# A fused recurrence, MLP and gated-MLP kernel: the first MLP group split by chunk, block two's first product in float16 parts, the state's outer product inside the values' step

## The chip, the cores and the metric

The kernel runs on one core of a Trainium2 chip. The metric is the device time of one execution in microseconds (us). TensorE, here PE, multiplies; its weight loads are shown as a separate row, PEld. VectorE is DVE, ScalarE is ACT, GpSimd is POOL, and SyncE, whose queue starts the DMAs, is SP.

## The reference

Three stages follow each other. Batch is 2, sequence 768, 8 heads of 48, so the model's width is 384.

```python
def _attn_ref(r, k, v, w, u):
    state = np.zeros((B, H, D, D))
    for t in range(S):
        cur = np.einsum('bhd,bhe->bhde', u[None] * kt, vt)
        y[:, :, t] = np.einsum('bhd,bhde->bhe', rt, state + cur)
        state = wt[:, :, :, None] * state + np.einsum('bhd,bhe->bhde', kt, vt)

def _moe_ref(x, g_ln, w_ch1, w_ch2):          # 384 -> 1536 -> 384
    xn = (x - mu) / np.sqrt(var + 1e-06) * g_ln
    return x + np.maximum(xn @ w_ch1, 0.0) @ w_ch2

def _moe2_ref(x, w_in, w_spatial, b_spatial, w_out):   # 384 -> 1024
    h = np.maximum(x @ w_in, 0.0)
    u, v = h[..., :512], h[..., 512:]
    v_n = (v - mu) / np.sqrt(var + 1e-06)
    v_s = np.einsum('ts,bsd->btd', w_spatial, v_n) + b_spatial[None, :, None]
    return (u * v_s) @ w_out
```

The weights arrive as float64, and the kernel makes float32 of their bits by itself.

## The kernel before

The sequence is cut into 6 chunks of 128 tokens. A step i stands for chunk c and batch b, i = 2c + b, so there are 12. For each i the recurrence is done in chunk form: `prep` scans the decays forward and backward on DVE (tiles `Gs` and `E`) and multiplies them with the keys and receptances; `keys_t` transposes the keys on PE (`kT`), and ACT copies them (`kf`); `scores` multiplies keys with receptances (`sc`), and DVE masks the result (`am`); `values` forms the output of the chunk, for the first chunk from `am` alone (`y<-tk,am`), for later ones in three pieces, `inter` from the state (`y<-E,St`) and `intra(0)` and `intra(1)` from `am` (`y<-am,tk`); `state` forms the outer product of keys and values of the chunk for the next chunk's state (`stp<-tk,kf`) in a PSUM bank of its own turn; `norm` adds the term of `u` (`x`) and normalises (`st`, `k_var`, `sd`, `rs`, `xn`), where `sd` is ACT's square root; `turned` transposes `x` and `xn` on PE (`xT`, `xnT`) and ACT copies them to `x2v` and, for the first chunk, to `xfirst`.

The MLP (`moe1`) runs in six groups, one for each chunk of both batches, 256 tokens at a time. A group goes over 12 slices f of the hidden width: three products up (`pup`), a relu on ACT (`hh`), three products down that add up in two PSUM banks (`acc`). Group 0 multiplies float32 (`xfirst`, `w1f`, `w2f`), which shows in the trace as two records for a product. Groups 1 to 5 split each operand into two float16 parts and take three float16 products for one.

The weights come in 24 pieces of 384 KB (`raw<-in_w`), first w1's slice 0, then w2's slice 0, and so on. `convert` makes float32 of a piece: a shift (on DVE or ACT), a rebias on ACT, a sign and a merge on DVE (`w1f`, `w2f`), and later the two float16 parts.

Block two then forms `v` (`v_tile`, 12 tiles of 9 products, 512 wide) and `u` (`u_tile`, 16 tiles of 9 products, 384 wide) from `x2v`, split into two float32r parts `Xh` and `Xl`, and `w_in`, split into `winh` and `winl`; it normalises v, multiplies with the spatial weights (`sp_tile`, `p<-ws,vn`, float16 parts) and with `w_out` (`o_tile`).

The order of the work is not the order of the code. Every step is given to a planner (`Plan.add`) with its engine, a cost, a key and what it reads and writes; `Plan.order` then takes on each engine, whenever it is free, the ready step with the lowest key, and writes the instructions out in that order. The keys come from the table `PP`. On PE the planner puts small products of zeros (`pw<-warm`, 128 x 128 float16) into the time before the first MLP product wherever PE would stand idle, so that PE's clock stays up. A few sums of range checks (`k_max`, `k_var`, `k_sum`) decide at the end whether a slow general version is run instead; with these inputs it isn't.

Of the kernel before, what the change touches and what calls it, by code (L numbers as in the profile page):

```python
# [8 lines left out]
F32 = mybir.dt.float32  # L9
# [36 lines left out]
W_UP = 2.0 ** 8  # L46
S_UP = 2.0 ** 15
# [8 lines left out]
PP = {'SK': 12.413, 'SS': -5.481, 'RG': 987.703, 'HK': 188.98, 'HS': 3.199, 'HW': 3.533, 'SG': 'V', 'T0': 18.217, 'P': 68.821, 'H': 29.796, 'H0': 3.345, 'M0': -20.127, 'M0S': 16.711, 'AH': 55.305, 'AG': -2.079, 'US': 6.83, 'EV': 33.376, 'CV': 3.765, 'CS': 12.226, 'CW': 3.915, 'WK': 602.422, 'WS': 70.654, 'XK': 12.678, 'XS': 39.166, 'KG': 18.972, 'KU': 578.872, 'OK': 564.596, 'OS': 13.4, 'FG': 108.0, 'LOOK': 0.0, 'EK': 'V', 'EU': 'V', 'ER': 'V', 'RK': 'V', 'ED': 'V', 'SM': 'V', 'SH': 'AAVVVAVAAVAVAVVVA', 'LW': 'V', 'LX': 'V', 'LS': 'V', 'LV': 'V', 'LU': 'V'}  # L56
# [287 lines left out]
def tile_rwkv_moe_gmlp(ctx: ExitStack, tc: tile.TileContext, dt_in, tok_in, vg_in, u_in, g_in, w1_in, w2_in, win_in, wsp_in, b_in, wout_in, out, plan_only=False):  # L344
# [79 lines left out]
    k_max = const.tile([128, 10], F32, name="k_max")  # L424
    k_sum = const.tile([128, NCH], F32, name="k_sum")
# [44 lines left out]
    def load_d(i, key):  # L470
# [10 lines left out]
        if i < B:  # L481
            for n, (lo, hi, w) in enumerate(((2 * NP * C, DTC, "dw"), (NP * C, 2 * NP * C, "dk"), (0, NP * C, "dr"))):
                add("D", 750, key + 0.01 * n, part(lo, hi, not n), w=[(w, s)])
        else:
            add("D", 2250, key, part(0, DTC, True), w=[("dw", s), ("dk", s), ("dr", s)])

    def load_k(i, key):
# [7 lines left out]
        add("D", 640 * n // DM, key, fn, w=[("tv", i % 2), ("tr", i % 2)])  # L495
# [23 lines left out]
    def set_ud():  # L519
        G.memset(ud, 0.0)  # L520

# [13 lines left out]
    add("G", 42, -95, set_ud, w=["ud"])  # L535
# [13 lines left out]
    def convert(name, src, n, key, hi, lo, r_hi=(), w_hi=(), r_lo=(), w_lo=(), shape=None, lo_eng="G", sh="A", sg="V", whole=None, later=None):  # L549
# [15 lines left out]
        def rebias():  # L565

            e = words()[0].bitcast(F32)
            A.activation(out=e, in_=e, func=ACTF.Copy, scale=REBIAS * 2 if whole else REBIAS)  # L568
# [173 lines left out]
    def scores(i):  # L742
# [17 lines left out]
        add("T", 1090, ka(i, "sc"), sc, r=[("E", s), ("G", s), "att"], w=pp, use=0.42)  # L760
# [4 lines left out]
    def values(i):  # L765
# [50 lines left out]
        add("T", 4 * 125, ka(i, "ya"), inter, r=[("E", s), ("St", b), "att"], w=py, use=0.5)  # L816
        for e in range(2):
            add("T", 4 * 125, ka(i, "yb"), intra(e), r=[t["amt", i][e], ("tv", s), "att"], w=py, use=0.39)
# [20 lines left out]

    def state(i):  # L840
# [4 lines left out]
        p = bank("up" if i == 0 else "ys")  # L845

        def st():
            z = t["stp", i] = pst(p, f"stp{i}_")
            for h in range(H):
                lo, hi = halves[h % 2]  # L850
                sl = slice(D * h, D * h + D)
                mm(z[lo:hi, D * (h // 2):D * (h // 2) + D], t["kf", i][:, h // 2, lo:hi], t["tk", i][:, sl], True, True)
# [4 lines left out]
        add("T", 600, ka(i, "st"), st, r=[("kf", s), ("tv", s), "att"], w=[p], use=0.3)  # L857
# [5 lines left out]
    def norm_steps(n, x, pool, key, cols, mv, tok, extra, w_mv=()):  # L863
# [535 lines left out]
```

## Time and profile before

| | us |
|---|---|
| time, median of 3 runs (359.56 to 360.32) | 359.74 |
| the profiled execution's own time | 362.65 |
| its span, from first to last instruction | 360.9 |
| PE busy in the span | 351.7 |
| DVE busy | 283.6 |
| ACT busy | 155.3 |

The profiled execution took 362.65 us, 1.75 us more than its span, and 2.9 us more than the median of the runs without the profiler. PE's busy share is an upper bound of its use, since the small products of zeros count too. The stages from the span's start: the load and the first chunk until 33 us, then the MLP's groups with the recurrence between them until about 242 us, and block two until 354 us.

### The profile page before, as it was taken

How to read it: one execution, taken by the hardware profiler on the slowest of the kernel's cores; microseconds unless marked ns; L12 is line 12 of the kernel's file. 1: busy time of each engine (PE TensorE's matmuls, PEld its weight loads, DVE VectorE, ACT ScalarE, POOL GpSimd, SP SyncE). 2: the span in 40 equal slices, each digit the busy share in tenths (PEclk: the TensorE clock that was granted, in tenths of full speed). 3: DMA queues.
4: the chain of work that ended last, by engine and by line, in shares of the span. 5: the costliest groups of instructions: out<-in, count | busy, mean ns of one | idle time of the engine just before them, and what ended most of it. 6: DMA issues, size and time to landing. Idle time of an engine off the chain costs nothing.

```text
span 360.9 us, 7549 instructions
## 1 busy us (share of the span) xinstructions
PE 351.7 (97%) x3041; PEld 298.8 (83%) x3041; DVE 283.6 (79%) x675; ACT 155.3 (43%) x364; POOL 2.2 (1%) x22
## 2 busy tenths in 40 slices
PE   8989999999999999999999999999999999999992
PEld 8989887779888888888889888889765899965692
DVE  7969999999999999999999999999255783025500
ACT  1557988333232332423544765663421354211121
POOL 1000000000000000000000000000000000000000
PEclk9989999999999999999999999999999999999998
DMA  8999796132222541320101026601000000210021
GB/s 211 295 307 360 232 312 201 33 112 67 77 67 78 145 129 41 119 67 31 59 31 60 30 74 200 194 3 44 3 2 0 2 0 2 79 54 2 0 84 58
DMA packets 13022, 34.85 MB, mean 97 GB/s; under 512 B 1840, under 2 KB 3888, under 8 KB 12976
## 3 DMA queue, kind: packets, MB, share of 16 engines
q1 hardware_dynamic: 12976, 34.26, 30.4%
q8 instruction: 26, 0.43, 0.5%
q14 instruction: 20, 0.16, 0.1%
HBM read 31.90 MB, written 2.36 MB: 95 GB/s over the span
## 4 chain that ended last, share of the span: by engine, by line
PE 89%; DMA 7%; ACT 1%; SPq 1%; issue 0%; DVE 0%; ACTq 0%
PE p L394 34%; PE acc L394 21%; DMA raw<-in_w 5%; PE sc L394 3%; DMA tk<-in_tok 2%; PE kT L717 1%; SPq L478 1%; PE pup__641 L394 0%; PE y__996 L394 0%; PE pup__930 L394 0%; PE pup__804 L394 0%; PE pup__1051 L394 0%; PE pup__981 L394 0%; PE pup__845 L394 0%; PE pup__773 L394 0%; PE pup__750 L394 0%
## 5 line engine op out<-in xcount | busy, mean ns | idle before, releaser
L394 PE MATMUL acc<-hh,w2h 128*128 128x256 f16 x180 | 49.2, 273 | 0.0
L394 PE MATMUL acc<-hl,w2h 128*128 128x256 f16 x180 | 49.1, 273 | 0.0
L394 PE MATMUL acc<-hh,w2l 128*128 128x256 f16 x180 | 49.1, 273 | 0.0
L394 PE MATMUL p<-ws,vn 128*128 128x384 f16 x288 | 47.1, 326 | 0.0
L394 PEld LDWEIGHTS <-vn 128*128 128x128 f16 x288 | 28.0, 98 | 18.7 <-issue 0.4
L394 PEld LDWEIGHTS <-w2h 128*128 128x128 f16 x360 | 33.9, 98 | 6.3 <-issue 2.2
L394 PEld LDWEIGHTS <-w1h 128*128 128x128 f16 x360 | 34.9, 98 | 4.3 <-issue 0.2
L1224 DVE SCALAR_TENSOR_TENSOR misc<-p,misc 128x384 f32<-128x384 f32 x16 | 8.9, 558 | 30.6 <-PE p L394 30.6
L385 ACT ACTIVATE gh<-misc 128x384 fp32r<-128x384 f32 x16 | 8.4, 523 | 41.2 <-DVE misc L1225 41.2
L568 ACT ACTIVATE raw<-raw 128x384 f32<-128x384 f32 (+1 forms) x40 | 20.8, 524 | 4.3 <-DMA raw<-in_w 4.3
L574 ACT ACTIVATE raw<-raw 128x384 uint32<-128x384 uint32 (+1 forms) x31 | 15.9, 512 | 11.9 <-DMA raw<-in_w 11.9
L585 DVE SCALAR_TENSOR_TENSOR raw<-raw 128x384 int32<-128x384 int32 (+1 forms) x40 | 20.2, 511 | 0.4 <-ACT raw L568 0.3
L394 PE MATMUL pw<-warm 128*128 128x128 f16 x259 | 19.0, 242 | 1.1 <-DVE warm L499 1.1
L394 PEld LDWEIGHTS <-w2l 128*128 128x128 f16 x180 | 17.6, 98 | 2.1
L394 PEld LDWEIGHTS <-w1l 128*128 128x128 f16 x180 | 17.6, 98 | 2.1
L394 PEld LDWEIGHTS <-warm 128*128 128x128 f16 x259 | 18.0, 111 | 1.2 <-DVE warm L499 1.1
L394 PE MATMUL acc<-hh,w2f 128*128 128x256 f32 x72 | 17.9, 385 | 0.0
L388 DVE TENSOR_TENSOR gl<-misc,gh 128x384 fp32r<-128x384 f32 x16 | 8.9, 558 | 9.4 <-ACT gh L385 9.4
L394 PE MATMUL p<-woh,gl 128*128 128x384 f32 x48 | 16.3, 340 | 0.0
L394 PE MATMUL p<-woh,gh 128*128 128x384 f32 x48 | 16.2, 337 | 0.0
L394 PE MATMUL p<-xh,winh 128*128 128x384 f32 x48 | 16.2, 337 | 0.0
L394 PE MATMUL p<-wol,gh 128*128 128x384 f32 x48 | 16.1, 336 | 0.0
(702 smaller groups left out, 911.4 us busy)
## 6 DMA issues: line engine op xcount, KB each, us to landing
raw<-in_w SPq DMA_DIRECT2D x24, 384.0 KB, 7.2
dt<-in_dt SPq DMA_DIRECT2D x10, 675.5 KB, 5.3
tk<-in_tok SPq DMA_DIRECT2D x10, 576.0 KB, 3.7
raw<-in_win SPq DMA_DIRECT2D x12, 256.0 KB, 3.1
raw<-in_wsp SPq DMA_DIRECT2D x6, 384.0 KB, 3.4
out<-misc SPq DMA_DIRECT2D x12, 192.0 KB, 1.9
raw<-in_wout SPq DMA_DIRECT2D x4, 384.0 KB, 3.4
dt<-in_dt SPq DMA_DIRECT2D x4, 224.0 KB, 5.2
```

The source lines that it names most:

```text
L385: A.activation(out=out, in_=in_, func=ACTF.Copy)
L388: eng[e].tensor_tensor(out=out, in0=in0, in1=in1, op=ALU.subtract)
L394: T.matmul(out=out, lhsT=lhsT, rhs=rhs, start=start, stop=stop)
L478: Q.dma_start(out=t["dt", i][:, lo:hi], in_=dt_in[b, c, :, lo:hi])
L568: A.activation(out=e, in_=e, func=ACTF.Copy, scale=REBIAS * 2 if whole else REBIAS)
L574: A.activation(out=z, in_=z, func=ACTF.Copy, scale=TOP3, bias=TOP3_BIAS)
L585: V.scalar_tensor_tensor(out=lw, in0=hw, scalar=SIGN, in1=lw, op0=ALU.bitwise_and, op1=ALU.bitwise_or)
L717: T.transpose(pv[:, j, 0:R], t["kt", i][:, j], ident[0:R, 0:R])
L1224: add("V", cv(384), key, lambda: V.scalar_tensor_tensor(out=tm_(), in0=t["spp", b, th, f][:, 0:384], scalar=1.0 / S_UP, in1=t["b"][:, ts], ...
```

## The change

There are three edits and a new table of keys.

1. Group 0 of the MLP becomes `moe0`: it treats the two batches' chunks j = 0 and 1 apart, 128 tokens at a time, each with its own keys, so that slices of j = 0 can run before the normalised x of batch 1 exists. The same weight slice is loaded into PE for either j. `k_max` and the other checks grow by a few entries.
2. Block two's first product takes float16 parts: `Xh`, `Xl`, `winh` and `winl` become float16, x is scaled by 4, the weights by 256, and the relu scales back. The new checks on DVE are `k_max` of `winh` (3 sums), the largest |x| (`k_x`, in the place of `k_sum`) and the variance of v (`k_v`). The check's verdict moves from batch 0 to batch 1.
3. The outer product of `state` is issued at the end of `intra(1)` of `values`, into unused columns of the same PSUM bank (`y<-tk,kf`), for the 8 steps i = 2 to 9. For i = 0 and 1 it stays a step of its own.

`ud`, a small table of u, is laid out by the host and loaded by one DMA instead of two with a memset on POOL. The new table also moves shifts of weight pieces from DVE to ACT (9 to 5 on DVE), and `moe0`'s keys, costs of some steps and a switch for the low parts' engine are added.

```diff
-PP = {'SK': 12.413, 'SS': -5.481, 'RG': 987.703, 'HK': 188.98, 'HS': 3.199, 'HW': 3.533, 'SG': 'V', 'T0': 18.217, 'P': 68.821, 'H': 29.796, 'H0': 3.345, 'M0': -20.127, 'M0S': 16.711, 'AH': 55.305, 'AG': -2.079, 'US': 6.83, 'EV': 33.376, 'CV': 3.765, 'CS': 12.226, 'CW': 3.915, 'WK': 602.422, 'WS': 70.654, 'XK': 12.678, 'XS': 39.166, 'KG': 18.972, 'KU': 578.872, 'OK': 564.596, 'OS': 13.4, 'FG': 108.0, 'LOOK': 0.0, 'EK': 'V', 'EU': 'V', 'ER': 'V', 'RK': 'V', 'ED': 'V', 'SM': 'V', 'SH': 'AAVVVAVAAVAVAVVVA', 'LW': 'V', 'LX': 'V', 'LS': 'V', 'LV': 'V', 'LU': 'V'}
+PP = {'SK': -0.827, 'SS': 132.363, 'RG': 650.856, 'HK': 159.604, 'HS': 10.95, 'HW': 13.936, 'SG': 'V', 'T0': 6.956, 'P': 73.293, 'H': 8.489, 'H0': 15.405, 'M0': -27.328, 'LO': 'V', 'E0': 1.326, 'E0S': 11.471, 'M0S': 19.862, 'AH': 53.324, 'AG': -122.95, 'US': 6.627, 'EV': 2142.356, 'CV': -10.438, 'CS': 19.696, 'CW': 17.088, 'WK': 4246.21, 'WS': 24.0, 'XK': 16.067, 'XS': 53.531, 'KG': -2.69, 'KU': 90.358, 'OK': -19.905, 'OS': 63.089, 'FG': 108.0, 'LOOK': 0.0, 'EK': 'V', 'EU': 'V', 'ER': 'V', 'RK': 'V', 'ED': 'V', 'SM': 'V', 'SH': 'AVVAAAVVAAAAAAAAAAVA', 'LW': 'V', 'LX': 'V', 'LS': 'V', 'LV': 'V', 'LU': 'V'}
...
     def load_u():
-        uv = u_in.rearrange("(p two d) -> two d p", two=2, d=D)
-        for a, (lo, hi) in enumerate(halves):
-            Q.dma_start(out=ud[lo:lo + D, a::2], in_=uv[a])
+        Q.dma_start(out=ud, in_=ud_in)
...
                     mm(out(h, l), l, t["am", i, e][:, pr], False, pr >= NP - 2)
+                if e and c < NC - 1:
+
+                    outer(i, t["y2", i][0][:, 2 * C:])
...
+    def outer(i, z):
+        t["stp", i] = z
+        for h in range(H):
+            lo, hi = halves[h % 2]
+            sl = slice(D * h, D * h + D)
+            mm(z[lo:hi, D * (h // 2):D * (h // 2) + D], t["kf", i][:, h // 2, lo:hi], t["tk", i][:, sl], True, True)
+
     def state(i):
...
-        add("T", 600, ka(i, "st"), st, r=[("kf", s), ("tv", s), "att"], w=[p], use=0.3)
+        if i < NT:
+            p = bank("up" if i == 0 else "ys")
+            add("T", 600, ka(i, "st"), lambda: outer(i, pst(p, f"stp{i}_")), r=[("kf", s), ("tv", s), "att"], w=[p], use=0.3)
+        else:
+            p = t["yt", i]
...
+    def moe0():
+        at = [bank("acc"), bank("acc")]
+
+        def key(f, j):
+            return ku(0, f) if j else T0 + PP["E0"] + PP["E0S"] * f
+
+        def up(f, j):
+            p, h = bank("up"), slot("hf", 4)
+
+            def mm_():
+                z = t["up", f, j] = pst(p, f"pup0_{f}_{j}_")
+                for k in range(KD):
+                    mm(z[:, 0:C], w1f[:, k, 128 * f:128 * f + 128], xfirst[:, k, C * j:C * j + C], k == 0, k == KD - 1)
...
+        def down(f, j, h):
...
+                    o = 256 * (d % 2) + C * j
+                    mm(t["acc", 0, d // 2][:, o:o + C], w2f[:, f, 128 * d:128 * d + 128], t["h", f, j], (f, j) == (0, 0) and d != 1, (f, j) == (KH - 1, B - 1) and d > 0)
...
-                t["win", k, j] = share.tile([128, 2 * DF], F32R, tag=big[2 * k + j][0], name=f"win{'hl'[j]}{k}")
+                t["win", k, j] = share.tile([128, 2 * DF], F16, tag=big[2 * k + j][0], name=f"win{'hl'[j]}{k}")
...
+            add("A", ca(DM), key, lambda sl=sl: A.activation(out=t["Xh"][:, :, sl], in_=x2v[:, :, sl], func=ACTF.Copy, scale=X_UP), r=[("x2", i), "p2"], w=[("Xh", i)])
...
+    for k in range(KD):
+        size(10 + k, lambda k=k: t["win", k, 0], [("winh", c0, k) for c0 in range(0, 2 * DF, 256)], 2 * DF)
```

How the order moves is read off the instructions as they stand on each engine, at three places.

The first is PE at the start of MLP group 0. Before, the first product up (`pup_0`) of both batches' 256 tokens stands behind the last products of zeros:

```order
L394 LDWEIGHTS warm
L394 MATMUL pw<-warm 128x128
L394 MATMUL pup_0__641<-xfirst,w1f 128x256 x3
L394 MATMUL pup_1__654<-xfirst,w1f 128x256 x3
L394 MATMUL acc_667<-hh,w2f 128x256 x2
L394 MATMUL acc_668<-hh,w2f 128x256
L394 MATMUL pup_2__681<-xfirst,w1f 128x256 x3
L394 MATMUL acc_667<-hh,w2f 128x256 x2
```

Now the first product up of slice 0 and batch 0 (`pup_0_0`, 128 tokens) stands right behind batch 1's transposed x (`xT`), and batch 1's normalised x (`xnT`) comes only after slices 0 to 2 of batch 0 and chunk 1's scores:

```order
L922 MATMUL xT__549<-ident,x_527 128x128 x3
L396 MATMUL pup_0_0__554<-xfirst,w1f 128x128 x3
L714 MATMUL kT_567<-ident,Gs_422 128x112 x4
...
L396 MATMUL pup_1_0__586<-xfirst,w1f 128x128 x3
L396 MATMUL acc_594<-hh,w2f 128x128 x2
L396 MATMUL acc_595<-hh,w2f 128x128
L396 MATMUL pup_2_0__607<-xfirst,w1f 128x128 x3
L396 MATMUL acc_594<-hh,w2f 128x128 x2
L396 MATMUL acc_595<-hh,w2f 128x128
L396 MATMUL sc_0_624<-E_572,Gs_422 128x128
L396 MATMUL sc_1_625<-E_572,Gs_422 128x128
...
L922 MATMUL xnT__641<-ident,xn_598 128x128 x3
```

What moved: batch 0's slices no longer wait for batch 1's normalisation, and chunk 1's recurrence steps (`kT`, `sc`) stand among the first slices instead of behind seven of them.

The second is ACT at the normalisation of the first chunk of batch 0, whose square root is `sd`. Before, the shift and the rebias of a further weight piece (lines 574 and 568) stand ahead of it:

```order
L568 ACTIVATE raw<-raw 128x384
L385 ACTIVATE St_110<-stp__424 112x192
L574 ACTIVATE raw<-raw 128x384
L568 ACTIVATE raw<-raw 128x384
L877 ACTIVATE sd<-k_var,eps_t 128x1
```

Now (line 571 is the shift, 565 the rebias):

```order
L387 ACTIVATE w1h<-w1f 128x3x128
L387 ACTIVATE kf_418<-kT_395 128x456
L571 ACTIVATE raw<-raw 128x384
L881 ACTIVATE sd<-k_var,eps_t 128x1
L565 ACTIVATE raw<-raw 128x384
```

What moved: counted from the start, the shift ahead of `sd` is that of the fifth weight piece; before it was that of the sixth, with its rebias.

The third is PE where `values` of step 2 (chunk 1, batch 0) ends. Before, a slice of the MLP's down products stands between the last of `intra(1)` and `state`:

```order
L394 MATMUL y_0__857<-am_1_843,tk_433 64x128
L394 MATMUL y_1__858<-am_1_843,tk_433 48x128
L394 MATMUL acc_667<-hh,w2f 128x256 x2
L394 MATMUL acc_668<-hh,w2f 128x256
L394 MATMUL stp__897<-tk_433,kf_808 64x48
L394 MATMUL stp__897<-tk_433,kf_808 48x48
```

Now the outer product follows at once, 8 products, and the down products stand behind it:

```order
L396 MATMUL y_0__653<-am_1_651,tk_456 64x128
L396 MATMUL y_1__654<-am_1_651,tk_456 48x128
L396 MATMUL y_0__653<-tk_456,kf_578 64x48
L396 MATMUL y_0__653<-tk_456,kf_578 48x48
...
L396 MATMUL acc_594<-hh,w2f 128x128 x2
L396 MATMUL acc_595<-hh,w2f 128x128
```

What moved: a change from full-size products to the small ones and back is gone from PE's row at this place.

## Rows read from the trace of the kernel before

**Rows 1.** windows (us; busy us of PE, PEld, DVE, ACT, POOL; granted clock, DMA)

```profile
33.00:354.20 321.20, 321.20 (x2653) 269.31 (x2650) 256.29 (x613) 139.71 (x330) 0.57 (x10) 1.00 0.25 78
```

**Rows 2.** waits of PE over the span: total us, times, longest

```profile
PE xnT__510 L918 <- ACT xn L907: 1.3, 1, 1.3
```

**Rows 3.** timeline, 20 to 33 us: start us, us, engine, line, operation

```profile
20.66 0.55 ACT L568 ACTIVATE raw<-raw 128x384 f32<-128x384 f32 x1 [1.56 <-DMA raw<-in_w]
...
23.63 0.55 ACT L574 ACTIVATE raw<-raw 128x384 uint32<-128x384 uint32 x1 [2.19 <-DMA raw<-in_w]
...
24.51 0.29 ACT L877 ACTIVATE sd<-k_var,eps_t 128x1 f32<-128x1 f32 x1
...
24.83 0.16 DVE L879 RECIPROCAL y<-sd 128x1 f32<-128x1 f32 x1 [2.31 <-ACT sd L877]
...
25.84 0.55 DVE L894 TENSOR_TENSOR x<-y__464,dv 128x384 f32<-128x384 f32 x1
...
27.42 0.53 PE L918 MATMUL xT__521<-ident,x 128*128 128x128 f32 x3
...
27.79 3.90 PE L394 MATMUL pw<-warm 128*128 128x128 f16 x67
...
32.99 1.56 PE L394 MATMUL pup__641<-xfirst,w1f 128*128 128x256 f32 x6
```

**Rows 4.** timeline, single DVE instructions of 20 to 31 us

```profile
27.24 0.55 DVE L590 SCALAR_TENSOR_TENSOR w1f<-raw 128x384 int32<-128x384 int32 x1
...
30.35 1.23 DVE L635 TENSOR_TENSOR_SCAN Gs<-dt,onehot 112x516 f32<-112x516 f32 x1
```

**Rows 5.** windows of 20 us, columns as in rows 1

```profile
80.00:100.00 20.00, 20.00 (x217) 17.54 (x216) 20.00 (x50) 6.05 (x16) 0.00 (x0) 1.00 0.21 65
...
260.00:280.00 20.00, 20.00 (x125) 12.05 (x124) 11.50 (x21) 3.66 (x7) 0.00 (x0) 1.00 0.00 1
```

**Rows 6.** timeline, weight loads (PEld) of float32 products

```profile
16.54 0.97 PEld L394 LDWEIGHTS kT<-ud,tk 112*128 112x128 f32 x8
...
17.43 0.97 PEld L394 LDWEIGHTS y__372<-tk,am 128*128 128x128 f32 x8
...
34.17 1.27 PEld L394 LDWEIGHTS pup__654<-xfirst,w1f 128*128 128x128 f32 x6
```

**Rows 7.** chain that ended last, 58 to 64 us: start us, us, what

```profile
58.77 0.60 PE stp__897 L394 x14
59.37 0.53 PE yT__912 L835 x4
59.90 0.38 PE kT L717 x4
...
61.59 1.09 PE sc L394 x16
62.69 1.49 PE acc L394 x6
64.18 1.29 PE pup__981 L394 x6
```

**Rows 8.** the same chain: chunk 1's first scores; a float16 group up

```profile
51.78 1.09 PE sc L394 x16
...
227.28 0.98 PE pup__3444 L394 x9
```

**Rows 9.** windows of v's tiles and u's tiles of batch 1

```profile
280.50:292.89 12.39, 12.39 (x57) 10.28 (x56) 9.79 (x29) 5.82 (x12) 0.00 (x0) 1.00 0.01 1
292.89:305.40 12.51, 12.51 (x74) 12.51 (x73) 7.01 (x23) 6.69 (x15) 0.00 (x0) 1.00 0.00 0
```

**Rows 10.** groups of PE instructions: line, operation, shapes, xcount | busy us, mean ns

```profile
L394 PE MATMUL p<-ws,vn 128*128 128x384 f16 x288 | 47.1, 326 | 0.0
```

**Rows 11.** window at half clock, columns as in rows 1

```profile
20.00:23.40 3.40, 3.40 (x36) 3.31 (x34) 2.53 (x7) 0.77 (x2) 0.00 (x0) 0.50 1.04 352
```

**Rows 12.** timeline of the end

```profile
354.31 0.49 ACT L385 ACTIVATE misc<-p 128x384 f32<-128x384 f32 x1 [1.61 <-PE p L394]
```

More of the change, by code (lines that the diff above doesn't have):

```diff
@@ L46 @@
 W_UP = 2.0 ** 8
+X_UP = 2.0 ** 2
+V_VAR = 2.0 ** -6
 S_UP = 2.0 ** 15
@@ L567, in rebias @@
             e = words()[0].bitcast(F32)
-            A.activation(out=e, in_=e, func=ACTF.Copy, scale=REBIAS * 2 if whole else REBIAS)
+            A.activation(out=e, in_=e, func=ACTF.Copy, scale=REBIAS * 2 if twice else REBIAS)
         def shift():
@@ L815, in values @@
         py = [p, bank("sc")]
[L816 removed]
+        add("T", 4 * 155, ka(i, "ya"), inter, r=[("E", s), ("St", b), "att"], w=py, use=0.5)
         for e in range(2):
[L818 removed]
+            new = e and c < NC - 1
+            add("T", 4 * 130 + (400 if new else 0), ka(i, "yb"), intra(e), r=[t["amt", i][e], ("tv", s), "att"] + ([("kf", s)] if new else []), w=py, use=0.39)
         def ys(j):
@@ L870, in bn @@
             z["st"] = pool().tile([128, 6], F32, tag=f"st{ln[1]}", name="st")
-            z["mv"] = k_var[:, mv] if mv is not None else pool().tile([128, 2], F32, tag=f"mv{ln[1]}", name="mv")
+            z["mv"] = (k_var if keep is None else keep)[:, mv]
             V.bn_stats(out=z["st"], in_=x())
@@ L932, in turned, with plus, added @@
         add("V", cv(DM), ka(i, "xnT"), lambda: sub("V", xring_l[:, :, o:o + C], pv("xn"), xring_h[:, :, o:o + C]), r=[pn, ("xh", q)], w=[("xl", q)], two=False)
+    def plus(z, y):
+        V.scalar_tensor_tensor(out=z, in0=y, scalar=W_UP ** -2, in1=z, op0=ALU.mult, op1=ALU.add)
+    def added(g, at, r0=(), r1=()):
+        xv = x2v.rearrange("q k (b c t) -> q k b c t", b=B, t=C)[:, :, :, g]
+        k = ku(g, KH) - PP["EV"]
+        x2 = [("x2", B * g + j) for j in range(B)]
+        add("V", cv(512), k, lambda: plus(xv[:, 0:2], t["acc", g, 0].rearrange("q (k b t) -> q k b t", k=2, b=B)), r=[at[0], *r0], w=x2, two=False)
+        add("V", cv(256), k, lambda: plus(xv[:, 2], t["acc", g, 1][:, 0:256].rearrange("q (b t) -> q b t", b=B)), r=[at[1], *r1], w=x2, two=False)
@@ L983, in fn @@
                     sl = slice(128 * d, 128 * d + 128)
-                    first, last = f == 0 and d != 1, f == KH - 1 and d > 0
-                    if not g:
-                        mm(acc(d), w2f[:, f, sl], hs[f][0], first, last)
-                        return
                     hh, hl = hs[f]
-                    mm3(acc(d), [(w2h[:, f, sl], w2l[:, f, sl], hh, hl)], start=first, stop=last)
+                    mm3(acc(d), [(w2h[:, f, sl], w2l[:, f, sl], hh, hl)], start=f == 0 and d != 1, stop=f == KH - 1 and d > 0)
                 return fn
@@ L1000, in moe1 @@
                 down(f - 1)
-        xv = x2v.rearrange("q k (b c t) -> q k b c t", b=B, t=C)[:, :, :, g]
-        k = ku(g, KH) - PP["EV"]
-        x2 = [("x2", B * g + j) for j in range(B)]
-        def plus(z, y):
-            V.scalar_tensor_tensor(out=z, in0=y, scalar=W_UP ** -2, in1=z, op0=ALU.mult, op1=ALU.add)
-        add("V", cv(512), k, lambda: plus(xv[:, 0:2], t["acc", g, 0].rearrange("q (k b t) -> q k b t", k=2, b=B)), r=[at[0]], w=x2, two=False)
-        add("V", cv(256), k, lambda: plus(xv[:, 2], acc(2).rearrange("q (b t) -> q b t", b=B)), r=[at[1]], w=x2, two=False)
+        added(g, at)
     def loads(i):
@@ L1367, in _pack @@
     tok = np.concatenate([tmajor(v), tmajor(r), tmajor(k)], axis=3)
+    uh = np.asarray(u).reshape(NP, 2, D)
+    ud = np.zeros((R, H), uh.dtype)
+    for a in range(2):
+        ud[64 * a:64 * a + D, a::2] = uh[:, a].T
     def words(x):
```

107 lines of the change are left out of this document (55 added, 52 removed).

## The prediction

> **What bounds the kernel now.** I read the windows first. From 33.0 us to the last product at 354.2 us PE is busy 321.20 of 321.20 us, and over the whole span the longest wait of PE for another engine is 1.3 us, before that stretch [rows 1, 2]. So the time is a sum: the moment at which the first MLP product starts (32.99 us [rows 3]), the products behind it, one after another, and the copy and store after the last [rows 12]. Whatever takes products away counts in full, and so does an earlier start, as long as the other engines keep up. Before 33 us PE is filled with products of zeros; a group of 67 of them runs 3.90 us until batch 1's normalised x arrives [rows 3]. That stretch is the prize. The view to fear is DVE's: 20.00 of 20.00 us in the window from 80 us [rows 5].
>
> **The start.** The first product now stands behind batch 1's transposed x, and needs batch 0's normalised x. Batch 0's chain: its square root ran at 24.51 us, since ACT had first to wait 2.19 us for the sixth weight piece (23.63 us), and DVE's reciprocal waited 2.31 us for it [rows 3]. Now it stands behind the fifth piece's shift, and the fifth was there for ACT at 20.66 us [rows 3]. So the square root comes 2.5 to 3.5 us earlier and DVE's 2.31 us of waiting go; batch 0 is then not what comes last. Batch 1's x started on DVE at 25.84 us. Ahead of it stand in the new order, beyond those of before, one scan (1.23 us [rows 4]), three instructions of the size of 0.55 us and a small one of 0.16 us, and one shift less, which I put at 0.4: 2.6 us net. So it starts at 25.84 - 2.31 + 2.6 = 26.1 us, takes 0.55, the transposes 0.53 [rows 3], and with the signals between them the first MLP product could start at 27.2 us. DVE and ACT can meet waits for pieces that the old order had not: up to 1.3 us. I take 27.8 us, a gain of **5.2 us** (4.5 to 5.8). The queue of DMAs has the same bytes ahead of the fifth piece, with one tiny load instead of two. The sixth piece now stands behind chunk 1's loads for batch 1 and batch 0's values. Who waits for it is slice 2's down product, which the order puts some 12 us behind the first product; its price is in the waits below.
>
> **The products.** (a) Float16 parts: batch 1's 54 products of v take 12.39 us, 229 ns each, and the 72 of u 12.51 us, 174 ns each [rows 9]. Float16 products of 384 columns take 47.1/288 = 163.5 ns [rows 10], of 256 columns 0.98/9 = 109 ns [rows 8], so 128 columns are 54.5 ns and 512 columns 218 ns. 108 products save 11.4 ns and 144 save 10.3 ns: **-2.7 us** (-2.2 to -3.2). (b) The halves: 72 float32 products of 256 columns take two records of 1.29/6 = 215 ns each, measured on down products and up products alike [rows 7]: 31.0 us. Now there are 288 records of 128 columns, 107.5 ns each if the columns alone count; but each brings its own weight load. Eight float32 loads started at 16.54 us and the next group's first at 17.43 us: 111 ns each, with next to nothing to multiply between them [rows 6]. The trace has no full-size float32 product of 128 columns; the nearest from above is the scores' group, 8 pairs of 128 columns in 1.09 us, 136 ns, with its entry [rows 7]. Bounds: 0 and +8.2 us. I take 111 ns, since the load's pace is the row with no other cause in it: 32.0 us, **+1.0 us**. (c) The state: in the old order the step cost 0.60 us, and four transposes behind it 0.53 us where four others took 0.38 [rows 7]: 0.15 us for the way back. I put the way in at 0.10 (0 to 0.20, the price of a full-size group behind the scores, 1.49 against 1.29 us [rows 7]). Eight steps: -2.0 us; I take **-1.8** (-0.6 to -2.8). The bank is no longer shared in turns, and the outer product now waits for ACT's copy of the keys, issued long before it. (d) The new order cuts the values' and the first MLP's groups at 4 or 5 more places, 0.20 us each: **+0.9** (0 to 1.5). (e) Behind the start, not before it, now run batch 1's three transposes of normalised x (0.5 us) and six products of zeros (3.90/67 = 0.06 us each [rows 3]): **+0.8**. Sum: -2.7 + 1.0 - 1.8 + 0.9 + 0.8 = **-1.8 us**.
>
> A sentence of the Trainium skill speaks against (b). What the trace shows: the loads of the second product up start at 34.17 us [rows 6], while the first one's group runs from 32.99 for 1.56 us to 34.55 [rows 3], in the same rows of the array. The Trainium skill ("TensorE: Matmul & The Clock Gate", Part 3) says that LDWEIGHTS overlaps with running matmuls "only when row_grp differs". By that rule the loads would lie open here, which is the second rival; the row does not agree with it.
>
> **The waits that come.** The attention of chunk 1 used to come 18 us after the first MLP product (its first scores stand at 51.78 us [rows 8]); now it follows at once, and DVE has to keep up. From batch 1's x to the first mask of chunk 1 the new order has 19 DVE instructions: two scans at 1.23 us, eight of some 0.6 and nine small ones of about 0.18: 8.9 us end to end, some 8 with their overlap. From 26.1 us this is 34.1. PE has until then three product groups up and two down of six records (0.67 each), the scores (1.09), transposes (0.38 and 0.53), zeros (0.4): 5.8 us, until 33.6. So PE waits half a microsecond there. Behind it stand 13 more DVE instructions before slice 2's w2 is merged, some 7 us, against 5.3 us of PE work: about 1 us more. With what I can't see (ACT behind late pieces, the load of the bias after the last range check) I take **+2.5 us**, between 0 and 5. The three new sums over `winh` are 3 times 1.2 us of DVE work; the guards and the verdict fall where DVE has 8.5 us of 20 free [rows 5] or are small, and four shifts go over to ACT: nothing, or 2 us if DVE has no gap left.
>
> **The sum.** -5.2 - 1.8 + 2.5 = -4.5 us; what lies behind the last product is unchanged. Against the profiled execution's own 362.65 us (span 360.9) this is 358.2. That execution is 2.9 us above the median of 359.74, and I take the difference to the median: about **355.4 us**.
>
> **Rivals.** (1) DVE takes the early start back: the recurrence is paced by DVE until 240 us, and PE, 5.2 us ahead at 28 us, waits for it all along. For it: DVE full [rows 5]; against it: PE never waited for DVE in this stretch, and some of DVE's work has late use. Only (a) stays, 357.0 us. (2) **Slower**: the weight loads of the halves lie open. Place: the 288 records of group 0; price: a load (111 ns) and columns (107.5) one after the other, 62.9 us instead of 32.0, so 386 us. It turns into a loss from (4.5 + 0.7)/288 = 18 ns a record beyond my 111, that is from 129 ns, which the scores' 136 ns would already pass. Against it: the overlap in rows 3 and 6. (3) The clock: from 20.0 to 23.4 us the granted clock was 0.50 [rows 11], 1.2 instead of 2.4 GHz, after a stretch of small products. If such a stretch falls on work that PE has to do, 3.4 us at half speed cost 1.7 us: 357.1. Fewer products of zeros (212 instead of 259) speak for it, the fuller start against. (4) No waits at all and a start at 27.2 us: 352.3. (5) A guard fails and the general version runs: many times the time; weights and variances give no reason.
>
> **How the numbers follow.** Chances: forecast 0.56, rival 1 0.16, rival 2 0.05, rival 3 0.11, rival 4 0.10, rival 5 and others 0.02. The range of 353.0 to 358.0 leaves out rival 2 and part of 4. A measurement tells 0.2%, 0.7 us, from no change. The forecast's bounds and rivals 1, 3 and 4 are faster by more: 0.91. Rival 2 begins with a zone of no change: same 0.04, slower 0.05.
>
> **What would show it.** In the changed profile: the first product up near 27.8 us (a start after 30 us refutes the order's reading); group 0's records at 111 ns; v's products near 218 and u's near 164 ns; waits of PE for DVE between 33 and 42 us of 1 to 3 us in sum, and few later; the outer product without an entry. The forecast is wrong if records of group 0 pass 129 ns or if PE's waits for DVE go on past 100 us.

## The result and the profile after

The changed kernel takes 356.99 us, median of 19 runs (355.19 to 359.77), against 361.05 us for the kernel before, measured alongside (359.56 to 364.88). The ratio is 0.988, with a 95% interval of 0.9854 to 0.9906, so some 4.3 us were gained; two repeats below gave 3.3 and 3.6 us. The ratios, here and below, leave out a few runs that took over 1.5% longer than the fastest at a lower granted clock. Forecast were 355.4 us against 359.74, a ratio of 0.988 too. The profiled execution of the changed kernel took 359.77 us, with a span of 358.1; that is the longest of its 19 runs, and 2.9 us less than the profiled execution of before.

From the first MLP product to the end of the last product. The windows' columns are as in [rows 1]: stretch, its length, busy PE, PEld, DVE, ACT, POOL, granted clock, DMA share and GB/s.

```profile
30.57:351.67 321.10, 320.14 (x2804) 257.22 (x2803) 261.17 (x624) 144.60 (x353) 0.68 (x12) 1.00 0.27 83
```

This answers to the window of [rows 1]. PE is still the bound: it is idle for 0.96 us of 321.10. Its waits over the span, which answer to [rows 2], are these:

```profile
PE y__502 L396 <- DVE am L754: 2.6, 1, 2.6
PE pw L396 <- DVE warm L502: 1.1, 1, 1.1
PE acc L396 <- DVE w2f L587: 0.7, 1, 0.7
PE y__654 L396 <- DVE am L754: 0.3, 1, 0.3
```

The longest is new: before the first MLP product PE waits 2.6 us for the mask of chunk 0, batch 1. The timeline of PE around it, the rows of ACT and DVE on which it turned, and PE's row of the first product, which answer to [rows 3]:

```profile
22.03 0.54 ACT L571 ACTIVATE raw<-raw 128x384 uint32<-128x384 uint32 x1 [2.87 <-DMA raw<-in_w]
22.48 0.28 ACT L881 ACTIVATE sd<-k_var,eps_t 128x1 f32<-128x1 f32 x1
...
22.79 0.16 DVE L883 RECIPROCAL y<-sd 128x1 f32<-128x1 f32 x1 [0.75 <-ACT sd L881]
...
24.05 1.28 DVE L754 TENSOR_TENSOR am<-sc,mask 128x512 f32<-128x512 f32 x2
...
24.79 1.51 PE L396 MATMUL y__502<-tk,am 128*128 128x48 f32 x8 [2.57 <-DVE am L754]
26.10 0.87 PE L922 MATMUL xnT__510<-ident,xn 128*128 128x128 f32 x3
26.76 1.78 PE L396 MATMUL y__502<-tk,am 128*128 128x48 f32 x8
28.34 1.80 PE L396 MATMUL pw<-warm 128*128 128x128 f16 x15
29.93 0.85 PE L922 MATMUL xT__549<-ident,x 128*128 128x128 f32 x3
30.57 1.49 PE L396 MATMUL pup__554<-xfirst,w1f 128*128 128x128 f32 x6
```

ACT waits for the fifth weight piece until 22.03 us, and its square root `sd` stands behind the piece's shift. On DVE the masks of batch 1 (`am`) now stand behind batch 0's reciprocal, which waits for that square root. In the kernel before they stood ahead of the reciprocal (24.83 us [rows 3]); the first of them:

```profile
20.60 0.68 DVE L757 TENSOR_TENSOR am<-sc,mask 128x512 f32<-128x512 f32 x1
```

In the changed kernel the first MLP product starts at 30.57 us: 2.4 us earlier than before, not the 5.2 that were forecast. The second half of the values takes 1.78 us for 8 records, and the windows show the granted clock there:

```profile
24.00:26.00 2.00, 1.21 (x8) 1.21 (x9) 2.00 (x6) 1.16 (x3) 0.00 (x0) 0.82 1.02 379
26.00:28.00 2.00, 2.00 (x12) 2.00 (x11) 1.28 (x4) 1.35 (x4) 0.00 (x0) 0.50 0.82 316
28.00:30.00 2.00, 2.00 (x19) 2.00 (x19) 1.42 (x4) 0.77 (x2) 0.00 (x0) 0.50 0.32 86
30.00:32.00 2.00, 2.00 (x12) 2.00 (x11) 2.00 (x6) 0.94 (x2) 0.00 (x0) 0.50 0.95 354
```

At 0.50 the clock is 1.2 instead of 2.4 GHz. In the kernel before such a stretch lay at 20.0 to 23.4 us [rows 11]; here it lies at the start of the MLP and is about twice as long.

The products themselves. First v's 54 and u's 72 products of batch 1, the windows that answer to [rows 9]; then, from the chain of work that ended last, what answers to [rows 7]:

```profile
278.72:290.38 11.66, 11.66 (x57) 5.29 (x55) 9.33 (x28) 4.95 (x10) 0.00 (x0) 1.00 0.01 1
290.38:302.08 11.70, 11.70 (x73) 6.94 (x71) 8.23 (x35) 7.33 (x16) 0.00 (x0) 1.00 0.00 1
```

```profile
52.93 0.46 PE y__822 L396 x16
53.39 0.48 PE xT__863 L922 x3
53.87 0.67 PE pup__869 L396 x6
...
59.06 0.33 PE xT__941 L922 x3
```

Six records of group 0 now take 0.67 us, 112 ns each. The joined outer product (`y__822`, 16 records) takes 0.46 us where the step of its own took 0.60; three transposes behind it take 0.48 us where the same elsewhere take 0.33, so the way back from small products to full-size ones still costs 0.15 us.

### The profile page after: what moved, and what is told of

It is laid out like the page before. It is cut to its first block, busy times and chain, and to the rows that moved or that the text cites. A ratio compares the mean times of both kernels' runs of the same rounds, so it can differ in the third digit from the quotient of the medians.

```text
span 358.1 us, 7770 instructions
## 1 busy us (share of the span) xinstructions
PE 347.0 (97%) x3138; PEld 283.1 (79%) x3138; DVE 285.8 (80%) x676; ACT 157.1 (44%) x380; POOL 2.3 (1%) x23
## 3 DMA queue, kind: packets, MB, share of 16 engines
q1 hardware_dynamic: 12688, 34.26, 31.1%
HBM read 31.90 MB, written 2.36 MB: 96 GB/s over the span
## 4 chain that ended last, share of the span: by engine, by line
PE 88%; DVE 5%; DMA 4%; ACT 1%; issue 0%; SPq 0%; ACTq 0%; DVEq 0%
PE p L396 33%; PE acc L396 21%; DMA raw<-in_w 3%; PE sc L396 3%; DVE Gs L632 1%; PE kT L714 1%; PE y__502 L396 1%; DMA dt<-in_dt 1%; DVE E L645 1%; DVE tk L393 1%; DVE am L754 1%; PE y__822 L396 1%; PE y__1465 L396 1%; PE y__2405 L396 0%; PE y__1928 L396 0%; PE y__2292 L396 0%
## 5 line engine op out<-in xcount | busy, mean ns | idle before, releaser
L571 ACT ACTIVATE raw<-raw 128x384 uint32<-128x384 uint32 (+1 forms) x35 | 18.3, 523 | 12.4 <-DMA raw<-in_w 12.3
L396 PE MATMUL acc<-hh,w2f 128*128 128x128 f32 x144 | 20.6, 277 | 0.7 <-DVE w2f L587 0.7
L396 PEld LDWEIGHTS acc<-hh,w2f 128*128 128x128 f32 x144 | 18.1, 192 | 1.1 <-issue 0.9
L632 DVE TENSOR_TENSOR_SCAN Gs<-dt,onehot 112x516 f32<-112x516 f32 x12 | 14.7, 1223 | 2.7 <-DMA dt<-in_dt 2.7
L396 PE MATMUL pw<-warm 128*128 128x128 f16 x212 | 15.7, 241 | 1.1 <-DVE warm L502 1.1
```

Of the source, the lines that this page charges most:

```text
L396: T.matmul(out=out, lhsT=lhsT, rhs=rhs, start=start, stop=stop)
L571: A.activation(out=z, in_=z, func=ACTF.Copy, scale=TOP3, bias=TOP3_BIAS)
L632: V.tensor_tensor_scan(out=g[:, n:0:-1], data0=d_()[:, 2 * NP * C + n:2 * NP * C:-1], data1=onehot[:, n:0:-1], initial=0.0, op0=ALU.mult, ...
```

## The experiments

Every kernel was run beside the kernel before on the same chip, and kernels of different groups of runs are compared by their ratios to it. Where a kernel was profiled, the table at the end of this section has its start and its length.

### What ended the start: the fifth piece, the mask, the clock

The changed kernel again, as the level.

> The changed kernel once more, as the level for the others of this call. Its one profile so far shows TensorE idle for 2.57 us before the values of chunk 0, batch 1, then a granted clock of 0.50 from about 25.5 to 32 us, and the first MLP product at 30.57 us instead of my 27.8. Theory A, the half clock is what came on top, and not every execution has it: over all executions span and mean granted clock go together (353.4 us at 0.998, 358.1 at 0.988), and one with a clock of 0.995 or more starts the MLP near 28 us. Rival, the start at 30.6 us is set by the order of the work on VectorE, and the clock only decides how fast TensorE waits: then the first product stands at 30 to 31 us in this profile too, whatever its clock. Time 4.3 us below the kernel before by both.

It took 357.3 us, ratio 0.9909 (0.9874 to 0.9943), and a second time, in a later group of runs on another chip (`a_level`), 357.4 us, ratio 0.99 (0.9868 to 0.9932).

> The changed kernel again, as the level for this call: about 4 us below the kernel before.

The profile of `a_again` starts the MLP at 29.00 us, not at 30.57. Six profiles have the same order of work up to that point: these two, the changed kernel's first one, and three kernels below that change only later work. Read from their timelines (us):

| profile | fifth piece's shift starts | PE waits for the mask | values start | half clock behind it | first MLP product |
|---|---|---|---|---|---|
| changed kernel | 22.03 | 2.57 | 24.79 | until about 32 | 30.57 |
| a_again | 21.34 | 1.65 | 24.11 | until about 29 | 29.00 |
| a_level | 21.16 | 1.75 | 23.93 | until about 29.5 | 28.23 |
| a_f32r | 21.17 | 1.38 | 23.95 | none | 27.74 |
| a_state_step | 20.33 | 0.96 | 23.11 | none | 26.56 |
| a_quarter | 21.60 | 1.51 | 24.36 | none | 27.82 |

The values start 2.76 to 2.78 us after the piece's shift in all six. So the arrival of that piece, through ACT's square root and DVE's masks, sets the start; and it varies by 1.7 us between executions. From the values to the first product it is 3.45 to 3.79 us at full clock, and 4.3 to 5.8 with the half clock. The expectation's theory A (the half clock comes on top) and its rival (the order sets the start) thus both hold a part: an execution without the half clock starts at 26.6 to 27.8 us, where 27.8 was forecast.

Does the idle time in front take the clock down? 40 products of zeros were put where PE waits.

```diff
+                    for _ in range(40 if i == 1 else 0):
+                        mm(t["pw"][:, 0:128], t["warm"], t["warm"], True, True)
```

> The changed kernel with 40 more products of zeros (56 ns each, 2.2 us in all) ahead of the values of chunk 0, batch 1, where TensorE waited 2.57 us; nothing else moves. Theory A, the idle stretch is what takes the clock down: the granted clock stays 1.0 through 25 to 32 us, the 16 products of these values take 1.9 us instead of 3.5, the first MLP product comes at 28.0 us, and the time falls by 2 to 3 us below the changed kernel's in executions that had the half clock, about 1.5 in the median. Rival, the small products of this stretch take it down, as at 20.0 to 23.4 us in the kernel before, where TensorE had no idle time ahead: the clock falls to 0.50 as before and the time is the same within 0.5 us, or up to 2 us worse where the wait is shorter than the filling.

The profile has PE without a wait before the values and the clock at 1.00 all along:

```profile
22.89 2.56 PE L396 MATMUL pw<-warm 128*128 128x128 f16 x43
25.31 1.09 PE L396 MATMUL y__502<-tk,am 128*128 128x48 f32 x8
...
26.59 0.99 PE L396 MATMUL y__502<-tk,am 128*128 128x48 f32 x8
```

```profile
26.00:28.00 2.00, 2.00 (x26) 2.00 (x26) 2.00 (x6) 1.55 (x4) 0.00 (x0) 1.00 0.53 200
28.00:30.00 2.00, 2.00 (x25) 1.86 (x23) 2.00 (x5) 1.85 (x5) 0.00 (x0) 1.00 0.74 233
```

But the time was 358.06 us, ratio 0.9937 (0.9901 to 0.9972): nothing gained, and 2.46 us of PE's waits behind the first product instead of 0.95. In this execution the fifth piece let ACT go at 22.53 us, the latest of all; the values came 2.78 us behind it and the first product, at 28.76 us, 3.45 us behind those, the pace of the executions at full clock. Over its 12 runs the mean clock was 0.994 against 0.992 for the 12 of `a_again`. So the one profile has no half clock, which fits the idea that the wait takes it down but does not show it: three of the six profiles above have none either, without the filling. And it did not shorten the kernel; theory A's gain of 1.5 us did not come. The largest of PE's later waits, 1.6 us until 42.99 us, was for a relu of ACT behind the shift of a weight piece for which ACT had waited 3.1 us; whether the filling had a part in that was not separated.

The other way is to take the wait's cause away. One ACT instruction was moved: the shift of the fifth piece stands behind the square root.

```diff
+    step = order.pop(names().index(mark[('shift', ('w1', 2))]))
+    order.insert(names().index(mark[('sd', ('x', 0))]) + 1, step)
```

> The changed kernel with one ACT instruction moved: the shift of the fifth weight piece stands behind the square root of chunk 0, batch 0, not ahead of it. In four profiles of the changed kernel and its variants the fifth piece let ACT go at 20.33, 21.17, 21.34 and 22.03 us, and the first MLP product came at 26.56, 27.74, 29.00 and 30.57 us. Theory B, the arrival of that piece sets the start by way of the square root: without it the reciprocal on VectorE, which waited 0.75 to 1.2 us, follows the scan at once, the first product comes 0.75 to 1.2 us earlier at the same arrivals, TensorE's wait for the mask shrinks from 1.4 to 2.6 to about 1 us, and the time falls by about 1 us, more where the clock then holds. Rival, later pieces set the pace: the gain at the start is given back as waits of TensorE before 60 us and the time stays within 0.4 us.

> The kernel with the shift of the fifth weight piece behind the square root once more, for its level. Theory B: about 1 us below the changed kernel (0.988 to 0.991 of the kernel before so far), that is 0.985 to 0.988, with a mean granted clock near 0.995 instead of 0.992. Rival: 0.989 to 0.991, nothing gained.

Two sets of runs gave 355.98 us, ratio 0.989 (0.985 to 0.993), and 355.7 us, ratio 0.9881 (0.9851 to 0.9911). In the first set's profile (ACT, then PE) the square root no longer waits for the piece, and neither do the values:

```profile
19.14 0.29 ACT L885 ACTIVATE sd<-k_var,eps_t 128x1 f32<-128x1 f32 x1
20.18 0.58 ACT L573 ACTIVATE raw<-raw 128x384 uint32<-128x384 uint32 x1 [0.75 <-DMA raw<-in_w]
```

```profile
22.18 1.09 PE L396 MATMUL y__502<-tk,am 128*128 128x48 f32 x8
...
25.76 0.83 PE L396 MATMUL pup__554<-xfirst,w1f 128*128 128x128 f32 x6
```

The first MLP product comes at 25.76 us and the last product ends at 346.38 us, the earliest of all profiles; but in this execution the piece itself came early, at 20.18 us. Against 2.77 us behind the piece's shift, where the values stood in the six profiles above, they start 0.8 us earlier in the first set's profile and 1.1 us in the second's (shift 22.36, values 24.02 us), the size that theory B gave, 0.75 to 1.2 us. In the second set's profile the values still waited 1.1 us for the mask, and the transposes of x another 1.0 us for DVE, which gives most of that back. The mean granted clock of the second set was 0.996, as theory B expected. The ratios 0.989 and 0.9881 lie among the changed kernel's three (0.988, 0.9909, 0.99), and the second lies between what theory B and its rival gave. So the mechanism is shown, and a gain in time is not.

With the first scan of chunk 1 behind the masks as well:

```diff
+    step = order.pop(names().index(mark[('scan', 2)]))
+    order.insert(names().index(mark[('am', 1, 1)]) + 1, step)
```

> As before, and on VectorE the first scan of chunk 1 (1.23 us, and 0.4 to 1.6 us of waiting for its table) stands behind the masks of chunk 0, batch 1, not ahead of the reciprocal. Theory B: the masks come 2.5 to 3 us earlier, TensorE waits for them less than 0.5 us, its clock stays at 1.0, and the first MLP product comes at 25.0 to 26 us. The scan and what hangs on it come no later than now, so 1 to 2 us of this should be left at the end: 355.5 us against the changed kernel's 357.2. Rival, the weight pieces: seven and more land at 26 to 30 us whatever the order, TensorE waits for slice 2's weights before 45 us, and nothing is left.

355.9 us, ratio 0.9898 (0.9862 to 0.9934). The wait moved; it did not go:

```profile
PE xT__549 L928 <- DVE start L644: 1.3, 1, 1.3
PE acc L396 <- DVE w2f L589: 0.7, 1, 0.7
```

The first product came at 26.99 us, not at the 25 to 26 us expected, and between the 25.76 and 28.45 us of the two profiles with the piece's shift alone; against their ratios nothing was gained. DVE has the same work ahead of batch 1's x in either order, and in this profile it also waited 0.67 us for a load of tokens.

### What each edit is worth

Block two's parts in float32r again, everything else as changed:

```diff
-        t["Xh"] = p2["w"].tile([128, KD, B * S], F16, name="xh")
+        t["Xh"] = p2["w"].tile([128, KD, B * S], F32R, name="xh")
```

(the same for `Xl` and `win`)

> The changed kernel with the parts of block two's first product in float32r again, in the same order. By the prediction's term (a) this costs 2.7 us (2.2 to 3.2): 108 products of 229 instead of 216 to 218 ns, 144 of 174 instead of 163. Since TensorE sets the time all through block two it should be seen in full: 1.6 us faster than the kernel before instead of 4.3. Rival, the order of block two has slack that hides it: the same time as the changed kernel.

359.59 us, ratio 0.9998 (0.9966 to 1.003). v's 54 products take 12.43 us again:

```profile
276.71:289.14 12.43, 12.43 (x57) 10.28 (x56) 9.57 (x29) 5.30 (x11) 0.00 (x0) 1.00 0.01 1
```

From the first MLP product on, the kernel is 323.51 - 320.37 = 3.1 us longer than `a_again`. The edit's gain is seen in full, as term (a) said, and it is as large as all that `a_again` gained (3.3 us by the ratio).

The state's outer product as a step of its own:

```diff
-                if e and c < NC - 1:
-                    outer(i, t["y2", i][0][:, 2 * C:])
...
-        if i < NT:
+        if i >= 0:
```

> The changed kernel with the state's outer product as a step of its own again for all chunks, so that the planner places it. By the prediction's term (c) this costs 1.8 us (0.6 to 2.8): eight steps of 0.60 us where eight outer products at the end of the values took 0.45 each, and eight ways back to the transposes at 0.10 to 0.15. Until the first MLP product nothing moves. Rival, the joined step gains nothing, since its wait for the keys' copy and its place cost what the switch saves: 0 within 0.5 us, or a gain.

Its ratio is 0.9991 (0.9951 to 1.003). From the first MLP product on it takes 323.23 us, 2.9 more than `a_again`; PE is busy for 321.64 instead of 319.42 us of that, so 2.2 us are products and 0.6 waits. Term (c) held.

Group 0 over both batches' 256 tokens again, with the new table:

```diff
-    mm(z[:, 0:C], w1f[:, k, ...], xfirst[:, k, C * j:C * j + C], k == 0, k == KD - 1)
+    mm(z[:, 0:2 * C], w1f[:, k, ...], xfirst[:, k], k == 0, k == KD - 1)
```

> The changed kernel with group 0's products over both batches' 256 tokens again, in the new table's order otherwise. Theory, the split is what makes the early start possible: the first product needs batch 1's normalised x (its transposes stand at 36.65 us in the changed kernel, and can come at about 32), so it starts at 31 to 33 us, 3 to 5 us later; its products cost 1 us less (72 of 430 ns against 144 of 223). The time is 2 to 4 us above the changed kernel's. Rival, the table and the other two edits bring the gain: the same time within 0.7 us.

356.6 us, ratio 0.9892 (0.9843 to 0.9941): the same as the split kernel. The expectation of 2 to 4 us more fell. Its first MLP product starts at 36.00 us (31 to 33 was expected), 3 us later than in the kernel before, and all behind it is shorter. The window from there to the last product, and what PE does ahead of it:

```profile
36.00:349.83 313.83, 313.83 (x2608) 247.55 (x2606) 255.44 (x608) 138.20 (x330) 0.68 (x12) 1.00 0.24 78
```

```profile
29.50 3.01 PE L396 MATMUL pw<-warm 128*128 128x128 f16 x51
32.45 1.16 PE L396 MATMUL sc<-E,Gs 64*128 64x128 f32 x16
...
34.39 0.50 PE L922 MATMUL xnT__679<-ident,xn 128*128 128x128 f32 x3
...
36.00 1.56 PE L396 MATMUL pup__708<-xfirst,w1f 128*128 128x256 f32 x6
```

The scores and values of chunk 1 run while PE would otherwise multiply zeros, and PE never waits afterwards. The split kernel starts the MLP 7 us earlier and is 320.37 us from there: the same end.

So are the two other edits the whole gain? The unsplit kernel with the table of before:

```diff
-PP = {'SK': -0.827, ..., 'T0': 6.956, ...}
+PP = {'SK': 12.413, ..., 'T0': 18.217, ...}
```

> The changed kernel without the split of group 0 and with the table of keys of the kernel before; what is left of the change is block two's float16 parts, the joined outer product, the guards and the single load of u. Theory C, these two edits are the whole gain (2.7 and 1.8 us in the prediction, 2.8 and 2.0 by taking them back), and the early start only pays for its own price (5.2 us against 1.0 + 0.9 + 0.8 + 2.5): the first MLP product stands at 32 to 33 us as before the change, and the time is that of the changed kernel within 0.7 us, 4 to 5 us below the kernel before. Rival D, the split with its table is worth something of its own: 1 to 3 us slower than the changed kernel.

358.81 us, ratio 0.9953 (0.9936 to 0.9971): some 1.7 us gained, not 4.3. PE's waits behind the first product, and the stretch in which they lie:

```profile
PE acc L396 <- DVE va L882: 1.5, 1, 1.5
PE yT__1155 L836 <- DVE xring_l L390: 1.4, 1, 1.4
...
PE y__1106 L396 <- DVE am L754: 0.5, 1, 0.5
PE xnT__1243 L922 <- ACT x2v L387: 0.4, 1, 0.4
```

```profile
70.00:90.00 20.00, 16.07 (x165) 12.81 (x164) 19.64 (x53) 6.55 (x16) 0.00 (x0) 1.00 0.21 65
```

With the old keys the planner, given the new steps, leaves PE waiting 3.9 us, most of it for DVE, between 70 and 90 us, where the new table leaves no wait. The last product ends at 352.03 us; less these waits it would be 348.1, against 349.83 of the unsplit kernel with the new table. From the first product on PE is busy for 317.48 us, 3.8 us less than before. So most of the products that the two edits save (5.3 us by taking them back, above) are saved under the old table too, and there they are lost again to waits, mainly for DVE. Theory C held for the products in the main and fell for the time. It fell at the start too: the first product came at 30.62 us, not at 32 to 33, as early as in the changed kernel's first profile and without the split. In this order the square root stands ahead of a shift, not behind it:

```profile
21.75 0.28 ACT L881 ACTIVATE sd<-k_var,eps_t 128x1 f32<-128x1 f32 x1
21.93 0.55 ACT L571 ACTIVATE raw<-raw 128x384 uint32<-128x384 uint32 x1
```

Without the split, and with the fifth piece's shift behind the square root:

> Without the split, with the new table, and with the shift of the fifth weight piece behind the square root. Its unsplit relative had its first product at 36.0 us and 356.6 us. Theory B, the square root's wait costs about 1 us here as well, and the half clock behind it another 1: 355 to 355.6 us, the lowest so far. Rival, without the split the first product waits for batch 1's normalised x anyway, other pieces decide, and the time stays at 356.6 us within 0.5.

356.27 us, ratio 0.9873 (0.9851 to 0.9895), with 313.83 us from the first product (35.05 us) on, to the hundredth as in `a_unsplit`. The first product came 0.95 us earlier than there, as theory B expected, but the time did not reach its 355 to 355.6 us and lies within the rival's 356.6 us, give or take 0.5. It is the lowest ratio of all, but its interval contains the changed kernel's 0.988.

### What sets the price of a float32 record

> The changed kernel with each product up of group 0 in two of 64 columns: 144 instead of 72, two records each, the same columns in all. If a weight load sets the pace of a float32 record (the 111 ns of my term (b)), each of the 144 further records costs 111 ns again: 16 us longer, 373 us, and records at 111 ns. If the columns do (107.5 ns for 128), records take 54 ns and the time stays the same within 1 us. If loads and columns lie one after the other, a record of 128 columns would have taken 219 ns already, which the changed kernel's 111.6 excludes.

```diff
+                    for q in range(2):
+                        mm(z[:, 64 * q:64 * q + 64], ..., xfirst[:, k, C * j + 64 * q:C * j + 64 * q + 64], ...)
```

370.32 us, ratio 1.0286 (1.0224 to 1.0348): 13 us longer than `a_again`. In the timeline of PE the group of 12 records of 64 columns runs from 31.90 to 33.18 us:

```profile
31.17 0.89 PE L396 MATMUL acc<-hh,w2f 128*128 128x128 f32 x6
31.90 1.45 PE L396 MATMUL pup__613<-xfirst,w1f 128*128 128x64 f32 x12
33.18 0.89 PE L396 MATMUL acc<-hh,w2f 128*128 128x128 f32 x6
```

That is 107 ns a record, with half the columns of the 112 ns in the changed kernel. The 144 further records cost 144 x 0.107 = 15.4 us; from the first product on the kernel is 14.6 us longer than `a_again`, whose 0.95 us of waits it no longer has. So the columns do not set the pace of such a record. The weight load, which each record brings along, fits: 111 ns in [rows 6]. Another cost of the same size that each record might have was not separated from it. The loads run beside the products before them, in the changed kernel too: PEld, and PE's row for the same time:

```profile
34.02 0.74 PEld L396 LDWEIGHTS pup__607<-xfirst,w1f 128*128 128x128 f32 x6
```

```profile
33.43 0.83 PE L396 MATMUL acc<-hh,w2f 128*128 128x128 f32 x6
34.10 0.85 PE L396 MATMUL pup__607<-xfirst,w1f 128*128 128x128 f32 x6
```

The loads start at 34.02 us, the products ahead of them end at 33.43 + 0.83 = 34.26. The Trainium skill ("TensorE: Matmul & The Clock Gate", Part 2, "LDWEIGHTS (loading the stationary operand)") gives a load's time as its columns divided by 1.2, in ns; for 128 columns this makes an estimate of 107 ns. The measured 107 to 112 ns agree.

### Starts and lengths

First MLP product, end of the last product, and the length between, from the windows and timelines (us):

| kernel | first product | last product ends | length | PE idle in it | ratio to before |
|---|---|---|---|---|---|
| before | 32.99 | 354.23 | 321.24 | 0.00 | 1 |
| changed | 30.57 | 351.67 | 321.10 | 0.96 | 0.988 |
| a_again | 29.00 | 349.37 | 320.37 | 0.95 | 0.9909 |
| a_level | 28.23 | 349.16 | 320.93 | 0.96 | 0.99 |
| a_fill | 28.76 | 350.94 | 322.18 | 2.46 | 0.9937 |
| a_f32r | 27.74 | 351.25 | 323.51 | 0.93 | 0.9998 |
| a_state_step | 26.56 | 349.79 | 323.23 | 1.59 | 0.9991 |
| a_sd | 25.76 | 346.38 | 320.62 | 0.91 | 0.989 |
| a_sd_again | 28.45 | 348.87 | 320.42 | 0.93 | 0.9881 |
| a_sd_scan | 26.99 | 347.41 | 320.42 | 0.93 | 0.9898 |
| a_unsplit | 36.00 | 349.83 | 313.83 | 0.00 | 0.9892 |
| u_oldtable | 30.62 | 352.03 | 321.41 | 3.93 | 0.9953 |
| u_sd | 35.05 | 348.88 | 313.83 | 0.00 | 0.9873 |
| a_quarter | 27.82 | 362.80 | 334.98 | 0.00 | 1.0286 |

## Why the prediction was right, and where it was not

**The total** was right, 0.988 forecast and measured, and luck had a part in it. The start gave less than its 5.2 us and the waits took less than their 2.5, and the two errors offset each other. In microseconds the changed kernel took 356.99, 1.6 more than the 355.4 forecast, since the kernel before took 361.05 alongside and not the 359.74 of its first three runs; the repeats came to 0.9909 and 0.99. For the profiled execution 358.2 us were forecast and 359.77 came. The prediction's 0.91 for a faster kernel should be 0.93 by the chances that it adds up.

**The start** (27.8 us, bounds 27.2 to 28.5) is the term that was mis-sized in that execution. The chain was read rightly: the first product stands behind batch 1's x, and batch 0's square root behind the fifth piece's shift. What failed is the use of 20.66 us [rows 3] as that piece's time: it was one arrival in one execution, and in the six profiles above it lay between 20.33 and 22.03. The square root, which the prediction took as freed, was still the link that passed each delay on: the prediction counted DVE's work ahead of batch 1's x as one sum and did not say that batch 1's masks had moved behind batch 0's reciprocal, which still waited 0.75 us. The second cause is the clock, rival 3, which was to take 1.7 us once: in the first profile the half clock lasts from about 25.3 to 32 us and slows the values, the transposes and the first MLP products. From the values to the first product it is 5.8 us there against 3.45 to 3.79 without it, and PE's busy time behind that is 0.7 us more than in `a_again`. Without it the start came at 26.6 to 27.8 us. By the prediction's own sign, a start after 30 us, the first profile speaks against its reading of the order; the other five of the table, at 26.6 to 29.0 us, do not.

**The products** came out at the foretold size. From the first product on, `a_again`, with the half clock over when its MLP starts, is 0.87 us shorter than before with 0.95 us of waits in it, so its products are 1.8 us less; forecast were 1.8. By parts: (a) 54 products of v went from 12.39 to 11.66 us and 72 of u from 12.51 to 11.70, 13.5 and 11.3 ns each, 3.1 us in all (2.7 forecast, within its bounds). (b) 48 groups of 0.67 us are 32.2 us against 31.0, +1.2 (forecast 1.0); the choice of the load's 111 ns as the row to go by was right, and the scores' 136 ns were the wrong neighbour. (c) is worth 2.2 us by taking it back (forecast 1.8), though not all for the reason given: the way back of 0.15 us stayed and now lies on the transposes behind the joined product; saved are 0.14 us of the step itself and a way from the small values to the MLP's products and back. Six MLP records behind the step of its own took 0.86 us in `a_state_step` where six elsewhere take 0.67, so one such way costs some 0.2 us; that it makes up the rest of the 2.2 us is an estimate. What is left for (d) and (e) is -1.8 + 3.1 + 2.2 - 1.2 = 2.3 us, against 1.7; it is a remainder, not a measurement.

**The waits** were put at 2.5 us (0 to 5) and came to 0.96 us, at places that were named: 0.3 us for a mask at 37.85 us, and 0.7 us for slice 2's w2. DVE kept up better than the count of its instructions said, and rival 1 did not come: from 60 us on PE never waits.

**The balance of the split** stood in the prediction's own figures, and it did not say so: 5.2 us at the start against 1.0 + 0.9 + 0.8 + 2.5 = 5.2 us for what the start costs. Measured, the start's price is 1.2 + 2.3 + 0.95 = 4.5 us. Its gain is 4.0 us between the profiles of before and of `a_again`, but the profiled execution of before was 1.6 us longer than the median of 19 runs. An estimate of the usual start takes the medians and subtracts the 1.75 us beyond the span and the time from the first product to the end of the span (327.9 us before, 326.8 in `a_again`): 30.7 to 31.4 us before and 28.4 to 28.9 after, a gain of 2 to 3 us. So the early start did not pay for its price in full. `a_unsplit` shows directly that the split brings nothing: 7 us later at the first product, the same time. What carries the gain of 3.3 to 4.3 us are the products that block two and the joined step no longer spend, 3.1 + 2.2 = 5.3 us by taking them back, and it needed the new table to reach the end of the kernel (`u_oldtable`). The prize that the prediction named, the stretch of zeros before 33 us, was not what paid: `a_unsplit` fills it with chunk 1's scores and values instead, to the same end. Rival 2, the exposed loads, was excluded by 112 ns a record; guards cost nothing that shows.

Left open: which of the table's keys takes away the waits at 70 to 90 us, and whether the wait for the mask alone brings the clock down. In the six profiles it fell in the three with the longest waits; in the kernel before [rows 11], in `u_oldtable` and in `u_sd` it fell at about 18 to 20 us, among small products and not behind a long wait, so a wait is not the only way to it.

## What to carry to other kernels

When an edit lets the main loop start earlier, write down everything that moves from before the start to behind it, and compare that sum with the gain before adding anything else: here the two were equal in the forecast's own figures, and the kernel without the split took the same time. An engine that takes a short link of the critical chain (a square root) behind an instruction that waits for a load passes on every delay of that load; one arrival time in one trace is a sample, not a constant. Before float32 products are cut into narrower ones, compare the columns' time with the weight load's: with weights of 128 columns nothing more was saved per record below 128 columns (107 against 112 ns).

## What the runs showed of the hardware

A float32 record of 64 columns with weights of 128x128 costs what one of 128 does, 107 against 112 ns. The same load, behind the same loads in its queue, let ACT go between 20.33 and 22.53 us. And the clock goes with much of the spread between runs of one kernel, though a late piece and the half clock can come together: of the 19 runs of the changed kernel the one with the highest mean granted clock, 0.998, took 355.19 us, and one at 0.988 took 359.77; the correlation over the 19 is -0.83.
